# Two transformer layers of windowed attention and MLP on one core: half of the normed rows move to GpSimd, three tiles change their places, and all queues are ordered anew

## The chip, the cores and the metric

The kernel runs on one NeuronCore of a Trainium2 chip, with inputs and output in HBM. The metric is the device time of one execution in microseconds; lower is better. A profile is one execution taken by the hardware profiler; its time is given beside the times of the runs without a profile.

## The reference

The input is `x`, 2048 rows of 512 numbers in bf16. Two kinds of sublayer alternate, each on the normed rows and with a residual:

```python
def _layernorm(x, axis=-1, eps=1e-5):
    m = jnp.mean(x, axis=axis, keepdims=True)
    v = jnp.var(x, axis=axis, keepdims=True)
    return (x - m) / jnp.sqrt(v + eps)

def _A_ref(x, wqkv, wo):                     # H = 32 heads of 16, window W = 256
    q, k, v = ...                            # from x @ wqkv
    scores = jnp.einsum("bhqd,bhkd->bhqk", q, k) * (Dh ** -0.5)
    mask = (idx[:, None] - idx[None, :] >= 0) & (idx[:, None] - idx[None, :] < W)
    p = _softmax(jnp.where(mask[None, None], scores, -1e9), axis=-1)
    return ... @ wo                          # p times v, heads side by side

def _B_ref(x, w1, b1, w2, b2):               # F = 1792
    h = _gelu(jnp.einsum("bsd,df->bsf", x, w1) + b1)
    return jnp.einsum("bsf,fd->bsd", h, w2) + b2

x = x + _A_ref(_layernorm(x), wqkv, wo)
x = x + _B_ref(_layernorm(x), w1, b1, w2, b2)
x = x + _A_ref(_layernorm(x), wqkv, wo)      # the same weights once more
x = x + _B_ref(_layernorm(x), w1, b1, w2, b2)
```

## The kernel before

The 2048 rows are 16 tiles of 128; with the two repetitions there are 32 tile steps `tau`, in 16 blocks `b` of two tiles. All weights and `X`, the residual rows, stay in SBUF. For each block the program has these parts, each made of small nodes:

- `lnq(b)` and `kv(b)`: statistics of the rows (`bn_stats` L587, `bn_aggr` L589, variance plus eps L593, `pow` on GpSimd L599), the normed row `xn` (L609), a DMA transpose of it into `xnTA` (L614; six tiles use TensorE, L621), then the Q, K and V products (L635) and their copies out of PSUM into `QT` and `Va` (L576 on VectorE or L578 on ScalarE) and `KT` (L669). `Vs` is `Va` shifted by 64 partitions, made by two DMAs (L684).
- `attention(b)`: up to ten visits. A visit computes 512 columns of scores for eight heads (L736), two exponentials of 128x1024 out of PSUM into `E` on ScalarE (L743), and masks on `E`'s edges (L764, VectorE or GpSimd). Two P·V products (`pv`, L786) follow, each one after five visits; its result is transposed into `OD` (L795), divided by its sums (reciprocal L799, product into `Nb` L803) and transposed back (L809). The output projection adds to `X` (L835). Then a second norm gives the rows for the MLP, transposed into `xnTB`.
- `mlp(J)`: ten jobs of two or four tiles. Fourteen W1 products (L635, `xnTB` as moving data), bias and gelu into `gT` on ScalarE (L866, or L858 on VectorE and L861 on ScalarE in pairs), then one W2 product per tile (L635), added to `X` plus the bias row (L874 on GpSimd, L878 on VectorE). In the second repetition a DMA stores the tile (L882).

Nothing is scheduled at run time. A list `_ORDER` of 3080 node numbers gives one order for the whole program, and each engine's queue is that list cut down to its own nodes; `_ALT` lists the nodes that run on their second engine (a mask on GpSimd instead of VectorE, a copy on ScalarE instead of VectorE); `_BANKS` gives the PSUM bank of each group of matmuls. Every engine works through its queue in order and waits on semaphores for what a node reads or overwrites. One queue, SyncE's, issues all DMAs.

```python
for i in _ALT:
    nodes[i]["eng"], nodes[i]["fn"] = nodes[i]["alts"][1]
...
e0 = (first[b] + g) * 512 % NE              # the place of visit g of block b in E
```

`E` is a ring of `NE` columns, 15 visits. `xn` has four places. `xnTB` has two places of four tiles, by the job's number; `gT` holds one job of four tiles or two of two.

Of the kernel before, what the change touches and what calls it, by code (L numbers as in the profile page):

```python
# [7 lines left out]
ALU = mybir.AluOpType  # L8
# [11 lines left out]
class _Sched:  # L20
# [386 lines left out]
def bass_interleave_layers__sliding_block__dense_activation_gelu__prompt_kernel(  # L407
# [26 lines left out]
    SCALE = float(Dh) ** -0.5  # L434
    EPS = 1e-5
    VW = Dh + 1
    NB = NT // 2
    RB = T // 2
    HK = P // 2
    NE = 15 * 512  # L440
    VR = 8
    KB = 4
    QR = 3
    NXN = 4
    NOD = 1
    NXB = 3
# [10 lines left out]
    with ExitStack() as kctx:  # L457
# [368 lines left out]
        for J, (t0_, n_) in enumerate(JOBS):  # L826
            for i in range(n_):
                job_of[t0_ + i] = (J, i)
# [119 lines left out]
```

## Time and profile before

| what | value |
|---|---|
| median of 3 runs | 450.0 us (449.41 to 451.96) |
| profiled execution | 450.2 us, of which its span 448.5 us |
| TensorE matmul busy | 418.6 us, 93% of the span |
| ScalarE busy | 385.9 us, 86% |
| VectorE busy | 345.9 us, 77% |
| GpSimd busy | 207.6 us, 46% |
| TensorE clock granted | 0.995 of full speed |

In the profile PE is TensorE (PEld its weight loads), DVE VectorE, ACT ScalarE, POOL GpSimd and SP SyncE; an engine with a q at its end is its sequencer. L609 is line 609 of the kernel before. A group's row has the line, engine, operation, written and read tiles, their shapes and its count; then its busy time, the mean duration of one in ns, and the idle time of the engine before it with what ended it. A row of the timeline has its start, its duration and, in brackets, the idle time before it. Matmuls are pipelined, so that a busy TensorE isn't a TensorE at its peak.

### The profile page before, as it was taken

How to read it: one execution, taken by the hardware profiler on the slowest of the kernel's cores; microseconds unless marked ns; L12 is line 12 of the kernel's file. 1: busy time of each engine (PE TensorE's matmuls, PEld its weight loads, DVE VectorE, ACT ScalarE, POOL GpSimd, SP SyncE). 2: the span in 40 equal slices, each digit the busy share in tenths (PEclk: the TensorE clock that was granted, in tenths of full speed). 3: DMA queues.
4: the chain of work that ended last, by engine and by line, in shares of the span. 5: the costliest groups of instructions: out<-in, count | busy, mean ns of one | idle time of the engine just before them, and what ended most of it. 6: DMA issues, size and time to landing. Idle time of an engine off the chain costs nothing.

```text
span 448.5 us, 16830 instructions
## 1 busy us (share of the span) xinstructions
PE 418.6 (93%) x7507; PEld 231.5 (52%) x7579; DVE 345.9 (77%) x641; ACT 385.9 (86%) x455; POOL 207.6 (46%) x232
## 2 busy tenths in 40 slices
PE   7997999998789997999999999999899999999997
PEld 4554756544444553554445454464454464344673
DVE  6989989889885688786699778876797487763952
ACT  2896999999989898789899999999788978898632
POOL 5464343272542584641856136824555134734222
PEclk9999999999999999999999999999999999999999
DMA  7796412103210103221021201011422024101001
GB/s 236 200 201 174 100 33 50 26 15 49 49 31 13 26 4 52 50 26 23 4 54 40 43 13 27 22 33 30 70 56 44 1 33 80 38 1 48 5 23 48
DMA packets 47972, 23.25 MB, mean 52 GB/s; under 512 B 33180, under 2 KB 47900, under 8 KB 47900
## 3 DMA queue, kind: packets, MB, share of 16 engines
q1 hardware_dynamic: 47900, 22.17, 22.9%
q8 instruction: 60, 0.98, 0.9%
q14 instruction: 12, 0.10, 0.1%
HBM read 8.00 MB, written 2.10 MB: 23 GB/s over the span
## 4 chain that ended last, share of the span: by engine, by line
PE 69%; ACT 13%; DVE 10%; DMA 4%; issue 2%; SPq 1%; POOL 1%; DVEq 0%
PE ps L635 52%; ACT E L743 11%; PE ps L786 8%; PE ps L736 8%; DMA xnTB<-xn 2%; DVE OD L795 2%; DVE KT L669 2%; DVE xn L609 1%; DVE stat L587 1%; DVE E L764 1%; ACT gT L866 1%; DMA xnTA<-xn 1%; SPq L614 1%; DVE X L835 1%; POOL rstd L599 1%
## 5 line engine op out<-in xcount | busy, mean ns | idle before, releaser
L743 ACT ACTIVATE E<-ps 128x1024 bf16<-128x1024 f32 x300 | 285.0, 1035 | 34.7 <-PE ps L736 33.7
L764 POOL TENSOR_TENSOR E<-E,mask 128x512 bf16<-128x512 bf16 (+2 forms) x100 | 110.0, 1112 | 75.4 <-ACT E L743 75.2
L635 PE MATMUL ps<-xnTB,W_sb 128*128 128x512 bf16 (+1 forms) x542 | 114.0, 338 | 4.0 <-DMA xnTB<-xn 1.8
L635 PE MATMUL ps<-W_sb,gT 128*128 128x512 bf16 x420 | 111.3, 380 | 3.1 <-issue 2.4
L635 PE MATMUL ps<-xnTA,Wqkv_sb 128*128 128x256 bf16 x512 | 74.9, 273 | 3.5 <-issue 1.3
L635 PEld LDWEIGHTS ps<-xnTB,W_sb 128*128 128x128 bf16 x560 | 52.1, 98 | 43.8 <-issue 4.3
L764 DVE TENSOR_TENSOR E<-E,mask 128x512 bf16<-128x512 bf16 (+2 forms) x136 | 63.2, 490 | 11.4 <-ACT E L743 11.2
L736 PE MATMUL ps<-QT,KT 32*128 32x128 bf16 (+3 forms) x1920 | 60.5, 231 | 9.8 <-ACT E L743 5.9
L635 PEld LDWEIGHTS ps<-W_sb,gT 128*128 128x128 bf16 x448 | 39.7, 97 | 42.6 <-issue 3.8
L874 POOL TENSOR_TENSOR Xb<-X,b2all 128x512 f32<-128x512 bf16 x32 | 38.3, 1205 | 48.0 <-DVE X L878 44.5
L736 PEld LDWEIGHTS ps<-QT,KT 32*128 32x128 bf16 x1920 | 28.4, 92 | 61.1 <-ACT E L743 39.3
L635 PEld LDWEIGHTS ps<-xnTA,Wqkv_sb 128*128 128x128 bf16 x512 | 47.2, 98 | 24.5 <-issue 3.7
L795 DVE STREAM_TRANSPOSE OD<-ps 128x1024 f32<-128x1024 f32 x32 | 39.8, 1244 | 20.4 <-PE ps L786 19.9
L866 ACT ACTIVATE gT<-ps,b1T 128x512 bf16<-128x512 f32 (+1 forms) x80 | 43.5, 605 | 9.5 <-PE ps L635 9.1
L858 DVE TENSOR_SCALAR gT<-ps,b1T 128x512 bf16<-128x512 f32 (+1 forms) x60 | 36.7, 635 | 13.0 <-PE ps L635 12.7
L786 PE MATMUL ps<-E,Va 64*17 64x128 bf16 (+3 forms) x1920 | 43.6, 230 | 2.3 <-DMA Vs<-Va 0.8
L587 DVE BATCH_NORM_STATS2 stat<-X 128x6 f32<-128x512 bf16 x64 | 43.0, 680 | 1.9 <-DMA X<-in_A_x_dram 1.4
L786 PE MATMUL ps<-E,Vs 64*17 64x128 bf16 (+3 forms) x1920 | 44.2, 230 | 0.0
L803 POOL TENSOR_TENSOR Nb<-OD,Rc 128x512 bf16<-128x512 f32 x26 | 27.9, 1075 | 34.6 <-DVE Rc L799 33.7
L786 PEld LDWEIGHTS ps<-E,Va 64*17 64x17 bf16 x1920 | 37.1, 84 | 12.3 <-issue 8.3
L669 DVE TENSOR_TENSOR KT<-ps,parmask 128x1024 bf16<-128x1024 f32 x32 | 38.6, 1211 | 3.7 <-PE ps L635 3.6
L635 PE MATMUL ps<-Wo_sb,OT 128*128 128x512 bf16 x118 | 37.2, 380 | 1.2 <-issue 0.6
(51 smaller groups left out, 357.3 us busy)
## 6 DMA issues: line engine op xcount, KB each, us to landing
Vs<-Va SPq DMA_DIRECT2D x64, 68.0 KB, 2.1
W_sb<-in_B_w_dram SPq DMA_DIRECT2D x4, 512.0 KB, 7.7
out_dram<-X SPq DMA_DIRECT2D x16, 128.0 KB, 1.8
X<-in_A_x_dram SPq DMA_DIRECT2D x3, 512.0 KB, 6.0
Wqkv_sb<-in_A_wqkv_dram SPq DMA_DIRECT2D x4, 256.0 KB, 5.1
W_sb<-in_B_w_dram SPq DMA_DIRECT2D x2, 384.0 KB
W_sb<-in_B_w_dram SPq DMA_DIRECT2D x1, 768.0 KB, 8.0
Wqkv_sb<-in_A_wqkv_dram SPq DMA_DIRECT2D x1, 512.0 KB, 7.0
```

The lines of the kernel that those rows point to most:

```text
L587: add("dve", lambda e, B, t=t, k6=k6: e.bn_stats(stat6[:, k6, :], X[:, t, :]), reads=["X%d" % t], writes=["st%d" % k6], key="bs%d" % (k + j))
L635: r = e.matmul(ps[:, B[g][0], cols], lhsT, rhs, start=st, stop=sp)
L669: add("dve", lambda e, B, g=g, i=i: e.tensor_tensor(out=KT[:, kb, 2 * i : 2 * i + 2].rearrange("p c m a q -> p a (c m) q"), in0=ps[:, B[g] ...
L736: x = e.matmul(ps[:, bk[r], o : o + n], KT[rows, kb, c, m].rearrange("p a q -> p (a q)"), QT[rows, c, q : q + n], start=True, stop=True)
L743: add("act", lambda e, B, g_=g_, gi=gi: e.activation(E[:, 2 * gi : 2 * gi + 2, e0 : e0 + 512], ps[:, B[g_][0] : B[g_][0] + 2, :], AF.Exp, ...
L764: fn = lambda e, B: e.tensor_tensor(out=Ew, in0=Ew, in1=Mw, op=ALU.mult)
L786: x = e.matmul(ps[32 * r : 32 * r + VW, B[g][par], c % 2 * 2 * P + lo : c % 2 * 2 * P + hi], V[rows, (2 * b + m // 2) % VR, c * HC + 2 * r ...
L795: add("dve", lambda e, B: e.transpose(OD[:, s].rearrange("p a c q -> p (a c q)"), ps[:, B[g][0] : B[g][0] + 2, :]), reads=["ps:" + g], wri ...
L803: return e.tensor_tensor(out=Nb[:, s, :].rearrange("p (k a d) -> p a k d", a=2, d=Dh), in0=sums[:, :, :, 0:Dh], in1=rc[:, :, :, None].to_b ...
L858: add("dve", lambda e, B, g=g, fc=fc: e.tensor_scalar(out=gT[:, fc, c0 : c0 + M], in0=ps[:, B[g][0], 0:M], scalar1=b1T[:, fc : fc + 1], sc ...
L866: add("act", lambda e, B, g=g, fc=fc: e.activation(gT[:, fc, c0 : c0 + M], ps[:, B[g][0], 0:M], AF.Gelu_apprx_tanh, bias=b1T[:, fc : fc + ...
L874: add("pool", lambda e, B, t=t, xs=xs: e.tensor_tensor(out=Xb[:, xs, :], in0=X[:, t, :], in1=b2all[:], op=ALU.add), reads=["X%d" % t, "b2a ...
```

## The change

- The normed row (L609) gets GpSimd as a second engine. With the new `_ALT` 35 of the 64 rows are written by GpSimd and 29 by VectorE. In 21 pairs of tiles each engine writes one row, in seven pairs GpSimd writes both.
- `xnTB` is one tile of eight places, one for each tile step modulo 8, instead of two halves by job. `gT` has eight places instead of four, by the same rule.
- `E` has 11 visits instead of 15, and 64 columns of padding at the end of each row.
- `_ORDER`, `_ALT` and `_BANKS` are new. Of the other nodes with two engines, GpSimd does 115 masks instead of 100 and 24 divisions of P·V instead of 26; VectorE does 17 Q copies instead of 15, and four of the six copies of rows that TensorE transposed instead of three.

Matmuls, exponentials, gelu and DMAs are the same in number and shape.

```diff
 _ORDER = [
...
 _ALT = [
...
 _BANKS = [
...
-    NE = 15 * 512
+    NE = 11 * 512
...
-        xnTB = sb("xnTB", [P, 2, DC, 4 * P])
+        xnTB = sb("xnTB", [P, DC, 8 * P])
...
-        E = sb("E", [P, RG, NE])
+        E = sb("E", [P, RG, NE + HK])
...
-        gT = sb("gT", [P, FC, 4 * P])
+        gT = sb("gT", [P, FC, 8 * P])
...
-            add("dve", lambda e, B: e.tensor_scalar(
+            fx = lambda e, B: e.tensor_scalar(
                 out=xn[:, s, :], in0=X[:, t, :], scalar1=statmv[:, k, 0:1], scalar2=rstd[:, k : k + 1],
-                op0=ALU.subtract, op1=ALU.mult),
-                reads=["X%d" % t, "mv%d" % k, "rs%d" % k], writes=["xn%d" % s], key="xn%d" % k)
+                op0=ALU.subtract, op1=ALU.mult)
+            add("dve", fx, reads=["X%d" % t, "mv%d" % k, "rs%d" % k], writes=["xn%d" % s], key="xn%d" % k,
+                alt=(("pool", fx),))
...
-            layernorm(b, 1, [(xnTB[:, J % 2], i * P, "xb%d_%d" % (J % 2, i)) for J, i in (job_of[2 * b], job_of[2 * b + 1])])
+            layernorm(b, 1, [(xnTB, t % 8 * P, "xb%d" % (t % 8)) for t in (2 * b, 2 * b + 1)])
...
-            js = J % 2
             tau0, n = JOBS[J]
             M = n * P
-            h = J % 2 if n == 2 else 0
-            c0 = h * 2 * P
-            gn = lambda fc: ["g%d_%d" % (fc, i) for i in ((0, 1) if n == 4 else (h,))]
-            xr = ["xb%d_%d" % (js, i) for i in range(n)]
+            x0 = tau0 % 8 * P
+            c0 = x0
+            gn = lambda fc: ["g%d_%d" % (fc, (tau0 // 2 + i) % 4) for i in range(n // 2)]
+            xr = ["xb%d" % ((tau0 + i) % 8) for i in range(n)]
...
-                pe_group(g, [(W1_sb[:, dc, fc * P : (fc + 1) * P], xnTB[:, js, dc, 0:M], slice(0, M), dc == 0, dc == DC - 1)
+                pe_group(g, [(W1_sb[:, dc, fc * P : (fc + 1) * P], xnTB[:, dc, x0 : x0 + M], slice(0, M), dc == 0, dc == DC - 1)
```

More of the change, by code (lines that the diff above doesn't have):

```diff
@@ L821, in attention @@
                 outproj(2 * b + j)
-            layernorm(b, 1, [(xnTB[:, J % 2], i * P, "xb%d_%d" % (J % 2, i)) for J, i in (job_of[2 * b], job_of[2 * b + 1])])
+            layernorm(b, 1, [(xnTB, t % 8 * P, "xb%d" % (t % 8)) for t in (2 * b, 2 * b + 1)])
         od_rr = [0]
-        job_of = {}
-        for J, (t0_, n_) in enumerate(JOBS):
-            for i in range(n_):
-                job_of[t0_ + i] = (J, i)
         def outproj(tau):
```

361 rows, old and new, of tables (_ALT, _BANKS, _ORDER) are left out of this document.

## The prediction

> **What bounds the kernel now.** I read the page's busy times first, then the busy times of seven stretches whose borders are places where TensorE begins a P·V product (the last one of blocks 1, 2, 4, 5, 6 and 7), then the groups by form, then the timeline and the chain at the places where a stretch loses time.
>
> ```profile
> span 448.5 us, 16830 instructions
> PE 418.6 (93%) x7507; PEld 231.5 (52%) x7579; DVE 345.9 (77%) x641; ACT 385.9 (86%) x455; POOL 207.6 (46%) x232
> ```
>
> ```profile
> core 0: us, PE busy (x) PEld busy (x) DVE busy (x) ACT busy (x) POOL busy (x), PEclk, DMA share, GB/s
> 0.00:51.40 51.40, 44.52 (x696) 27.90 (x701) 45.76 (x88) 37.62 (x45) 26.28 (x43) 1.00 0.77 198
> 51.40:82.20 30.80, 30.34 (x547) 20.37 (x550) 27.50 (x55) 29.76 (x42) 11.38 (x13) 1.00 0.15 31
> 82.20:128.20 46.00, 38.71 (x908) 20.73 (x917) 38.82 (x74) 42.84 (x50) 21.39 (x24) 1.00 0.20 38
> 128.20:160.60 32.40, 31.77 (x511) 16.34 (x516) 20.81 (x39) 30.07 (x35) 13.95 (x16) 1.00 0.09 18
> 160.60:181.70 21.10, 17.57 (x425) 8.79 (x426) 16.64 (x30) 19.11 (x22) 13.50 (x15) 0.92 0.26 41
> 181.70:217.50 35.80, 34.38 (x567) 18.15 (x573) 26.84 (x50) 31.99 (x37) 17.34 (x18) 1.00 0.19 25
> 217.50:448.50 231.00, 221.29 (x3865) 119.18 (x3903) 169.49 (x309) 194.54 (x229) 103.74 (x105) 1.00 0.17 35
> ```
>
> The page says TensorE, 93% busy, and the stretches say where the other 7% lie. TensorE is idle 6.9 us of the first 51.4, where VectorE is the busiest engine (45.76); 7.3 us of 82 to 128 and 3.5 us of 161 to 182, where ScalarE is (42.84 of 46.00, 19.11 of 21.10): blocks 3, 4 and 6 have few MLP matmuls to lay beside the exponentials. From 217.5 on TensorE is busy 221.29 of 231.00 us, and no other engine comes near. So the matmuls, which are the same in number and shape in both kernels, are a floor, and what a new order can win lies in three stretches. An engine that isn't late in one of them gives nothing.
>
> **The memory edits.** Counted in the queues written into the two kernels, no more than eight visits' exponentials are alive at once, before as after; 11 slots hold them as 15 do, and every score matmul already stands behind the P·V product that frees its slot. When the first W1 matmul of a job stands in TensorE's queue, at most five W2 matmuls of the job before it are still to come (four after the change), so the doubled inner activations and the eight places of the W1 rows are hardly used. I cost these at 0 and their cover is TensorE's own queue order; if I have overlooked a slot, a score would wait for one P·V product, about 1.4 us, and not repeatedly.
>
> **The normed rows.** VectorE loses 35 of 64, GpSimd gets them. In the same new plan GpSimd takes 15 more masks (115 for 100), VectorE two more divisions of P·V (8 for 6) and two more Q copies, ScalarE two fewer Q copies and one fewer copy of transposed rows.
>
> ```profile
> L609 DVE TENSOR_SCALAR xn<-X,statmv,rstd 128x512 bf16<-128x512 bf16 x64 | 28.5, 462 | 6.4 <-POOL rstd L599 4.8 <-DMA xnTA<-xn 0.9 <-DVE Va L576 0.6
> L764 POOL TENSOR_TENSOR E<-E,mask 128x512 bf16<-128x512 bf16 x51 | 59.6, 1171 | 30.8 <-ACT E L743 30.8
> L764 DVE TENSOR_TENSOR E<-E,mask 128x512 bf16<-128x512 bf16 x65 | 30.9, 488 | 4.8 <-ACT E L743 4.7
> L576 DVE CAST Va<-ps 128x512 bf16<-128x512 f32 x25 | 16.9, 683 | 2.6 <-PE ps L635 2.6
> L578 ACT ACTIVATE Va<-ps 128x512 bf16<-128x512 f32 x7 | 4.3, 610 | 0.0
> L593 POOL TENSOR_SCALAR rstd<-statmv 128x2 f32<-128x2 f32 x24 | 6.1, 252 | 53.9 <-DVE statmv L589 53.9
> L516 POOL TENSOR_SCALAR_AFFINE_SELECT mask<-mask 128x64 bf16<-128x64 bf16 x3 | 0.7, 236 | 0.1
> L521 POOL TENSOR_SCALAR mask<-mask 128x128 bf16<-128x128 bf16 x1 | 0.3, 297 | 0.1
> L501 POOL TENSOR_SCALAR_AFFINE_SELECT ident<-ident 128x128 bf16<-128x128 bf16 x1 | 0.3, 292 | 0.0
> ```
>
> No row shows the normed row on GpSimd. Below: its two small TENSOR_SCALAR rows (252 ns at 2 elements, 297 at 128) rise 0.36 ns an element, which gives 0.43 us at 512. Above: the mask of the same size with two inputs, 1.17 us. The one-input AFFINE_SELECT rows (236 at 64, 292 at 128) rise 0.88 ns an element and give 0.63 us. I take 0.65, since that is the row with the same traffic, one tile in and one out; both ends stay for the range. On GpSimd that makes 35 × 0.65 = 23 us and 15 × 1.17 = 18 us more, about 248 of 448 us: no bound as a whole. The Trainium skill ("GPSIMD Engine Reference", § 3.1 Elementwise — side-by-side cycle accounting) has a one-input loop at 1.03 cycles an element; an estimate from that page is 0.44 us and a start-up, which speaks for the lower half; no run so far shows it for this shape.
>
> First stretch. Up to the place where VectorE evacuates the last P·V of block 1, its new queue holds six normed rows fewer (6 × 0.46 = 2.8 us), two masks fewer (1.0), one V copy more (0.68) and two or three small instructions (0.3): 2.8 us less. What it would bring is seen where TensorE waits for VectorE:
>
> ```profile
> 34.64 2.08 DVE L764 TENSOR_TENSOR E<-E,mask 128x512 bf16<-128x512 bf16 x2
> 38.71 1.19 DVE L669 TENSOR_TENSOR KT<-ps,parmask 128x1024 bf16<-128x1024 f32 x1
> 39.99 0.41 DVE L609 TENSOR_SCALAR xn<-X,statmv,rstd 128x512 bf16<-128x512 bf16 x1
> 41.48 1.73 DVE L609 TENSOR_SCALAR xn<-X,statmv,rstd 128x512 bf16<-128x512 bf16 x2
> ...
> 34.33 1.64 POOL L764 TENSOR_TENSOR E<-E,mask 128x768 bf16<-128x768 bf16 x1 [2.08 <-ACT E L743]
> 40.75 1.15 POOL L764 TENSOR_TENSOR E<-E,mask 128x512 bf16<-128x512 bf16 x1 [0.87 <-ACT E L743]
> 41.86 1.20 POOL L874 TENSOR_TENSOR Xb<-X,b2all 128x512 f32<-128x512 bf16 x1
> ...
> 39.96 1.48 PE L635 MATMUL ps<-xnTA,Wqkv_sb 128*128 128x256 bf16 x10 [1.27 <-DVE KT L669]
> 44.99 0.26 PE L736 MATMUL ps<-QT,KT 32*128 32x192 bf16 x3 [0.26 <-DVE KT L669]
> ```
>
> The matmul at 39.96 waits 1.27 us for the K copy of 38.71. Two masks there took 2.08 us instead of 2 × 0.49, and two normed rows 1.73 instead of 2 × 0.41, both while GpSimd worked on SBUF tiles: a VectorE instruction of these kinds starts as it should and then holds on until GpSimd's is over. That cuts both ways. The change takes those rows off VectorE, but 21 of the 32 pairs are now split, one row on each engine, let go by the same `pow` on GpSimd. GpSimd, whose own queue it is, goes first, and VectorE's row then lasts 0.65 + 0.41, no less than the two did on VectorE. Stepping through the new queues there: GpSimd's masks stand without a break up to the end of the one of 34.33 (35.97), so VectorE's mask before the residual add again ends near 36.4 (34.64 + 2.08 = 36.72 now), the K copy starts at 38.5 (38.71), the split pair delays the evacuation after it by 0.6, but the two rows at 41.48 are gone. So the stretch gains between 2.8 us (all of it passes) and -0.6 us (all of it is lost to this). I take the middle, 1.2 us. What comes early in the stretch is handed on in full: from 51.4 to 82.2 TensorE is busy 30.34 of 30.80, then ScalarE holds the pace, and both only start sooner. In the stretch 82 to 128 the new ScalarE queue holds the same work, so its 7.3 us of idle TensorE stay.
>
> 160.6 to 181.7. ScalarE is the bound and loses one V copy there, 0.61 us, to VectorE, which is busy 16.64 of 21.10 and so has room for 0.68: gain 0.6. The two rows that the next MLP job waits for are split as above, at no gain.
>
> SyncE. One wait in the TensorE-bound part is a queue matter:
>
> ```profile
> 316.84 0.95 DVE E L764
> 317.79 1.09 SPq L882
> 318.93 1.20 SPq L614
> 320.18 2.04 DMA Vs<-Va
> 322.26 1.44 PE ps L786 x120
> ...
> 322.26 0.28 PE L786 MATMUL ps<-E,Va 64*17 64x256 bf16 x4 [0.82 <-DMA Vs<-Va]
> ```
>
> The shifted copy of V is issued behind an output store (L882) and a transpose (L614), and P·V of block 12 idles 0.82 us for it. In the new SyncE queue the second store stands after that copy, the transpose still before it. The copy is issued some 1.1 us sooner, and the wait goes: 0.8 us. Next late there would be its masks; the last of them that the chain shows ends at 317.79, well before.
>
> Sum: 1.2 + 0.6 + 0.8 = 2.6 us. The profiled execution took 450.2 us, 448.5 of them its span; 450.2 - 2.6 = **447.6 us**. Against the median of 450.0 that is 0.5% less. About 0.5% (2.25 us) is what a measurement of this kernel can tell from no change.
>
> **The rivals.** *All of it passes*: the 2.8 us, the 0.6, the 0.8, and about 1 of the 7.3 us in 82 to 128, where VectorE (38.82 of 46.00 busy) has five normed rows fewer and frees PSUM sooner: 450.2 - 5.2 = 445.0. For it: VectorE's load falls in every stretch. Against: the port waits above.
>
> *Nothing changes*: VectorE's gain is eaten by waits for GpSimd, other small waits move about, 450. For it: after 217.5 us there is nothing to win but 9.7 us of small gaps, and none is VectorE's alone.
>
> *Slower: the split pairs and GpSimd's in-order queue.* The mechanism is the one of 41.48: VectorE's row costs up to 1.24 us instead of 0.41, its masks too. If GpSimd's row costs 1.17, the four rows in front of GpSimd's masks for the first blocks push these 4 × (1.17 - 0.65) = 2.1 us back, the first P·V products of block 1 wait for them, and four split pairs add 4 × 0.83 = 3.3 us where 2.8 were saved: the first stretch gets 2.6 us longer, 82 to 128, with two or three more split pairs, about 1 us, and the other gains don't come: 450.2 + 3.6 = 453.8. It decides from about 1.0 us for GpSimd's row, or 0.8 us as the mean of VectorE's. For it: GpSimd gets busier just where it is in front of masks. The Trainium skill ("SBUF — State Buffer", § SBUF: two separate sides) states the rule behind it: the pair of ports that both engines use is locked for a whole instruction, and the other one blocks. By that rule, the trace agrees: 1.73 us for two rows of 0.41. Against it: half of VectorE's rows, which suffer from this, are gone.
>
> **How the numbers follow.** Forecast 0.42 (its own range 445.5 to 449.5, a little over half of it below 447.75), all passes 0.18, nothing 0.17, slower 0.23. Faster by over 0.5%: 0.24 + 0.18 = 0.42; within: 0.18 + 0.17 = 0.35; slower: 0.23. The range goes from 444.0, just under the best case, to 453.8, the slower case's own time; half of that case and a few per cent below are left out.
>
> **What would show it.** In the changed profile: 29 rows of L609 on VectorE and 35 on GpSimd at 0.43 to 1.17 us; the seven stretches, by their P·V products, with the first ending near 50.2 us, 82 to 128 as long as now, 161 to 182 0.6 shorter, and P·V of block 12 without a wait for Vs. A first stretch over 52 us, or VectorE rows of 0.8 us and more, says the port; a stretch after 217 that changes by over 2 us says that the order of the matmuls matters in a way which I don't see.

## The result, and the profile after

| | before | after |
|---|---|---|
| median | 450.98 us of 4 runs (449.41 to 452.58) | 464.49 us of 4 runs (464.08 to 465.64) |
| ratio | | 1.0317, 95% interval 1.0283 to 1.0350 |
| profiled execution | 450.2 us, span 448.5 | 464.22 us, span 462.5 |

The change makes the kernel 3.2% slower. The forecast was 447.6 us, and 464.5 lies outside its range. Ratios here and below leave out the runs in which the chip was in a slower state, one of the four of a_head_fast and two of the ten of a_old_tables. The page of the changed kernel, busy times first:

```profile
span 462.5 us, 16921 instructions
PE 429.9 (93%) x7579; PEld 231.2 (50%) x7579; DVE 345.9 (75%) x597; ACT 385.8 (83%) x452; POOL 294.8 (64%) x279
```

GpSimd has 87 us more than before (207.6), where the prediction expected 41. VectorE lost 35 rows and 15 masks and is as busy as before, since what stayed with it takes longer (below). (TensorE's two sums can't be compared: 72 of its 7579 matmul records are missing in the trace of before.) The seven stretches of the changed kernel, with borders at the same P·V products as those of before:

```profile
core 0: us, PE busy (x) PEld busy (x) DVE busy (x) ACT busy (x) POOL busy (x), PEclk, DMA share, GB/s
0.00:55.90 55.90, 45.43 (x701) 27.54 (x701) 45.57 (x84) 39.51 (x47) 44.00 (x53) 0.97 0.62 169
55.90:88.80 32.90, 32.38 (x556) 21.11 (x557) 26.02 (x48) 28.10 (x40) 15.53 (x15) 0.95 0.29 55
88.80:137.60 48.80, 41.19 (x918) 20.84 (x918) 41.82 (x72) 42.59 (x49) 28.09 (x25) 0.97 0.16 33
137.60:170.80 33.20, 32.42 (x524) 16.39 (x529) 21.25 (x36) 30.23 (x35) 25.48 (x22) 1.00 0.09 18
170.80:189.70 18.90, 16.02 (x426) 8.42 (x425) 17.40 (x32) 17.86 (x21) 14.91 (x14) 1.00 0.22 45
189.70:226.10 36.40, 35.70 (x577) 18.45 (x576) 25.17 (x42) 32.66 (x37) 25.47 (x23) 1.00 0.12 25
226.10:462.50 236.40, 226.78 (x3904) 118.43 (x3903) 168.62 (x285) 194.82 (x229) 141.36 (x130) 1.00 0.15 34
```

Against before the stretches are 4.5, 2.1, 2.8 and 0.8 us longer, 2.2 shorter, 0.6 and 5.4 longer: 14.0 together. The first, where a gain of 1.2 us was forecast, loses most, and GpSimd is busy 44.00 of its 55.90 us (26.28 of 51.40 before).

A part of this stands in the column PEclk, TensorE's granted clock. In the changed kernel's trace it falls to 0.5 at three places, for some 3.4 us each: from 26.0 and 56.7 us, behind the two waits for GpSimd's masks that the timeline below shows, and from 128.6 us, behind a wait of 1.04 us for a mask of VectorE. In the trace of before it falls once, from 177.9 us. What the lower clock takes away is 5.0 us in all against 1.7, so 3.3 of the 14.0 us. In the second stretch, in which TensorE hardly rests, it is 1.6 of the 2.1 us. Not every wait is followed by such a fall; the longest of the timeline below, 2.99 us, isn't.

The groups by form say what GpSimd is busy with:

```profile
L612 POOL TENSOR_SCALAR xn<-X,statmv,rstd 128x512 bf16<-128x512 bf16 x35 | 74.5, 2131 | 5.1 <-DMA xnTA<-xn 3.4
L768 POOL TENSOR_TENSOR E<-E,mask 128x512 bf16<-128x512 bf16 x63 | 73.5, 1167 | 44.1 <-ACT E L747 44.0
L768 DVE TENSOR_TENSOR E<-E,mask 128x512 bf16<-128x512 bf16 x53 | 29.9, 568 | 1.8 <-ACT E L747 1.5
L612 DVE TENSOR_SCALAR xn<-X,statmv,rstd 128x512 bf16<-128x512 bf16 x29 | 16.2, 566 | 12.2 <-POOL rstd L602 7.8 <-DMA xnTA<-xn 3.3 <-DVE E L768 1.0
```

L612 is the normed row (L609 before). One takes GpSimd 2131 ns, where the prediction took 650 and had 1170 as its upper end. The masks on GpSimd cost what they did (1167, before 1171). In the waits, TensorE's weight load for P·V (L786 before, L790 after) now stands for a GpSimd mask, which it hardly did; the columns are the total in us, the number of waits and the longest:

```profile
PEld ps L786 <- POOL E L764: 0.8, 2, 0.4
```

```profile
PEld ps L790 <- POOL E L768: 5.9, 3, 2.5
```

The first fence is before, the second after. The timeline of the changed kernel shows what stands ahead of these masks, and at the end how the W1 products of a later MLP job come late:

```profile
18.52 4.15 POOL L612 TENSOR_SCALAR xn<-X,statmv,rstd 128x512 bf16<-128x512 bf16 x2
22.64 1.79 POOL L768 TENSOR_TENSOR E<-E,mask 128x768 bf16<-128x768 bf16 x1
...
24.48 0.28 PE L790 MATMUL ps<-E,Va 64*17 64x256 bf16 x4 [1.91 <-POOL E L768]
...
50.50 2.08 POOL L612 TENSOR_SCALAR xn<-X,statmv,rstd 128x512 bf16<-128x512 bf16 x1
52.54 1.46 POOL L807 TENSOR_TENSOR Nb<-OD,Rc 128x512 bf16<-128x512 f32 x1
53.96 1.89 POOL L768 TENSOR_TENSOR E<-E,mask 128x512 bf16<-128x512 bf16 x2
...
51.42 1.67 DVE L768 TENSOR_TENSOR E<-E,mask 128x512 bf16<-128x512 bf16 x4
...
55.91 0.09 PEld L790 LDWEIGHTS ps<-E,Va 64*17 64x17 bf16 x4 [2.46 <-POOL E L768]
...
341.20 4.14 POOL L612 TENSOR_SCALAR xn<-X,statmv,rstd 128x512 bf16<-128x512 bf16 x2
...
343.35 4.16 SPq L618 DMA_TRANSPOSE xnTB<-xn  x2
...
348.70 1.67 PE L639 MATMUL ps<-xnTB,W_sb 128*128 128x512 bf16 x7 [2.99 <-issue]
```

Two rows hold GpSimd for 4.15 us, the mask of block 0 starts behind them at 22.64, and TensorE idles 1.91 us until 24.48. A row, a division and two masks end at 55.85, and the P·V product that ends the first stretch starts at 55.91, after its weight load has waited 2.46 us. From 341.20 on both rows of one pair are written by GpSimd, one after the other. Their transposes follow, the second of them is issued at 345.37 and takes up to 3.2 us to land, and W1 waits 2.99 us until 348.70.

### The profile page after: what moved, and what is told of

Read it like the earlier page. It is cut to its first block, busy times and chain, and to the rows that moved or that the text cites. A ratio compares the mean times of both kernels' runs of the same rounds, so it can differ in the third digit from the quotient of the medians.

```text
span 462.5 us, 16921 instructions
## 1 busy us (share of the span) xinstructions
PE 429.9 (93%) x7579; PEld 231.2 (50%) x7579; DVE 345.9 (75%) x597; ACT 385.8 (83%) x452; POOL 294.8 (64%) x279
## 5 line engine op out<-in xcount | busy, mean ns | idle before, releaser
L768 POOL TENSOR_TENSOR E<-E,mask 128x512 bf16<-128x512 bf16 (+2 forms) x115 | 126.4, 1111 | 65.8 <-ACT E L747 65.5
L639 PE MATMUL ps<-xnTB,W_sb 128*128 128x512 bf16 (+1 forms) x560 | 118.6, 341 | 4.5 <-issue 3.0
L639 PE MATMUL ps<-W_sb,gT 128*128 128x512 bf16 x448 | 120.3, 380 | 0.0
L639 PE MATMUL ps<-xnTA,Wqkv_sb 128*128 128x256 bf16 x512 | 76.8, 279 | 4.6 <-DVE OD L799 1.6
L612 POOL TENSOR_SCALAR xn<-X,statmv,rstd 128x512 bf16<-128x512 bf16 x35 | 74.5, 2131 | 5.1 <-DMA xnTA<-xn 3.4
L768 DVE TENSOR_TENSOR E<-E,mask 128x768 bf16<-128x768 bf16 (+2 forms) x121 | 67.1, 576 | 7.0 <-ACT E L747 6.6
L790 PE MATMUL ps<-E,Va 64*17 64x128 bf16 (+3 forms) x1920 | 44.0, 232 | 9.1 <-DVE E L768 2.7
L857 DVE TENSOR_SCALAR gT<-ps,b1T 128x512 bf16<-128x512 f32 (+1 forms) x60 | 37.0, 637 | 14.1 <-PE ps L639 13.5
L790 PEld LDWEIGHTS ps<-E,Va 64*17 64x17 bf16 x1920 | 36.8, 84 | 19.0 <-issue 7.5
L790 PE MATMUL ps<-E,Vs 64*17 64x128 bf16 (+3 forms) x1920 | 44.7, 232 | 0.0
L807 POOL TENSOR_TENSOR Nb<-OD,Rc 128x512 bf16<-128x512 f32 x24 | 25.9, 1079 | 23.0 <-DVE Rc L803 17.7
```

The lines of the kernel that those rows point to most:

```text
L612: fx = lambda e, B: e.tensor_scalar(out=xn[:, s, :], in0=X[:, t, :], scalar1=statmv[:, k, 0:1], scalar2=rstd[:, k : k + 1], op0=ALU.subtra ...
L639: r = e.matmul(ps[:, B[g][0], cols], lhsT, rhs, start=st, stop=sp)
L768: fn = lambda e, B: e.tensor_tensor(out=Ew, in0=Ew, in1=Mw, op=ALU.mult)
L790: x = e.matmul(ps[32 * r : 32 * r + VW, B[g][par], c % 2 * 2 * P + lo : c % 2 * 2 * P + hi], V[rows, (2 * b + m // 2) % VR, c * HC + 2 * r ...
L857: add("dve", lambda e, B, g=g, fc=fc: e.tensor_scalar(out=gT[:, fc, c0 : c0 + M], in0=ps[:, B[g][0], 0:M], scalar1=b1T[:, fc : fc + 1], sc ...
```

## The experiments

The questions were, first, whether the loss comes from the rows on GpSimd, from the new order or from the new places; then why a row costs 2.1 us; and last, what the plan is worth at the price that was assumed. "After" and "before" are the two kernels; ratios are to the kernel before on the same chip. Its medians there were 450.6 to 451.6 us.

**a_rows_dve.** After, all 64 normed rows on VectorE.

```diff
-_ALT = [..., 110, 156, 158, 241, ...]   # the 35 nodes of the rows among them
+_ALT = [...]                            # without them
```

> The changed kernel with all 64 normed rows on VectorE again, everything else (order, masks, places) as changed. Theory 1, that the 14 us come from the normed row's duration on GpSimd (2.13 us, not 0.65): the 35 x 2.13 = 74.5 us leave GpSimd, VectorE gets 35 x 0.41 = 14 us back, and the time is that of before or a little less, 446 to 452. Theory 2, that the new order and the 15 masks more on GpSimd are slow by themselves: 460 or more. Theory 3, that the new places of E, xnTB and gT cost something: 460 or more as well.

457.31 us, ratio 1.0140 (1.0072 to 1.0208). This is the number of none of the three theories. Taking the rows away from GpSimd recovers about half of the loss. What the other half is, this run alone doesn't show; the new queues then hold VectorE rows that weren't there when the order was made.

**b_rows_pool.** Before, with the same 35 rows on GpSimd and nothing else.

```diff
-            add("dve", lambda e, B: e.tensor_scalar(
+            fx = lambda e, B: e.tensor_scalar(
...
+            add("dve", fx, ..., alt=(("pool", fx),))
+_ALT = [...]                            # before's, and the 35 rows
```

> The kernel before with the same 35 normed rows on GpSimd, nothing else changed (old order, old masks, old places). Theory 1: the rows alone slow it at least as much as the change did, since its order isn't made for them: 464 to 475. Theories 2 and 3: under 456, since the new order and the new places aren't in it.

465.15 us, ratio 1.0333 (1.0253 to 1.0412), as theory 1 had it: the rows alone cost as much as the whole change. Its groups by form and its waits:

```profile
L610 POOL TENSOR_SCALAR xn<-X,statmv,rstd 128x512 bf16<-128x512 bf16 x35 | 76.9, 2200 | 1.4
```

```profile
PE ps L637 <- DMA xnTB<-xn: 5.7, 2, 3.4
PE ps L637 <- DMA xnTA<-xn: 2.5, 1, 2.5
PE ps L623 <- POOL xn L610: 2.2, 1, 2.2
PE ps L788 <- POOL E L766: 2.1, 3, 1.0
```

Here it is the products that use the late rows which wait (10.4 us in the first three lines, where the kernel before has 2.2), more than P·V behind late masks (2.1).

**a_const.** After, GpSimd's 35 rows subtract and multiply constants instead of the mean and the reciprocal deviation.

```diff
+            fp = lambda e, B: e.tensor_scalar(
+                out=xn[:, s, :], in0=X[:, t, :], scalar1=0.125, scalar2=0.5, op0=ALU.subtract, op1=ALU.mult)
...
-                alt=(("pool", fx),))
+                alt=(("pool", fp),))
```

> The changed kernel, whose 35 rows on GpSimd subtract and multiply by constants instead of by the row's mean and rstd (this leaves the norm of these rows out; queues, waits and shapes stay). If the two scalars read per partition make the 2.13 us, the row falls to between 0.43 and 0.65 us, and theory 1 says 446 to 450, what the prediction's sum says. If the row's duration stays at 2.1 us, two operations on 512 elements cost that on GpSimd whatever the scalars, and the time stays at 464. Theory 2: 460 or more whatever the row costs.

461.49 us, ratio 1.0223 (1.0164 to 1.0282), and a row still costs 1.94 us:

```profile
L615 POOL TENSOR_SCALAR xn<-X 128x512 bf16<-128x512 bf16 x35 | 67.6, 1937 | 5.6 <-DMA xnTA<-xn 3.6
```

So the scalars, one per partition, are a small part of the price: 0.19 us of 2.13, and 3 us of the time.

**a_old_tables.** After's tiles and places with before's three tables.

```diff
-_ORDER, _ALT, _BANKS = after's
+_ORDER, _ALT, _BANKS = before's
```

> The changed kernel's tiles (11 visits in E with padding, eight places of xnTB and gT) with the order, the engines and the banks of the kernel before. Theory 3: the places cost time, 455 or more. Theories 1 and 2: 450 within 0.5%, as the prediction has it (places at 0).

450.94 us, ratio 0.9973 (0.9930 to 1.0017). The eight places and the 11 slots cost nothing that can be seen, 0.2% at most; the theory that they bring waits has fallen.

**a_forms.** After, GpSimd's 35 rows in seven forms, five rows each: subtract and multiply or multiply and add with constants, multiply and add in either order with a value per partition, and single operations. The norm is left out on these rows.

```diff
+            XNP = [2, 4, 5, 7, 8, 9, 11, ...]               # the rows that GpSimd writes
+            q = XNP.index(k) % 7
+            # 0: -0.125, *0.5   1: *0.5, +0.0625   2: -0.125   3: *rstd
+            # 4: *rstd, +mean   5: +mean, *rstd    6: *0.5
```

> The changed kernel, in which the 35 rows on GpSimd take seven forms in turn, five rows each: subtract and multiply with constants; multiply and add with constants; subtract alone; multiply by a per-partition scalar alone; multiply and add with two per-partition scalars; add and multiply with two; multiply by a constant alone (the norm is left out of these rows; only the duration of each form is read). Theory 1a, that the order of operations subtract-then-multiply has no fast path on GpSimd while multiply-then-add has: 2.0 us for the first, 0.4 to 0.8 us for the second and fifth. Theory 1b, that any two operations on 512 elements cost 1.9 us: all two-operation forms at 1.9 to 2.1, the single ones at about 1. Theory 1c, that it is one element after the other whatever is done: all seven near 1.9.

One execution, 456.39 us. The timeline has the first row of the first six forms, in the order 0, 2, 1, 3, 4, 5:

```profile
10.44 1.95 POOL L618 TENSOR_SCALAR xn<-X 128x512 bf16<-128x512 bf16 x1
...
19.79 1.50 POOL L619 TENSOR_SCALAR xn<-X 128x512 bf16<-128x512 bf16 x1
21.36 0.62 POOL L618 TENSOR_SCALAR xn<-X 128x512 bf16<-128x512 bf16 x1
...
25.65 1.57 POOL L619 TENSOR_SCALAR xn<-X,rstd 128x512 bf16<-128x512 bf16 x1
...
41.52 0.89 POOL L618 TENSOR_SCALAR xn<-X,rstd,statmv 128x512 bf16<-128x512 bf16 x1
44.47 0.77 POOL L618 TENSOR_SCALAR xn<-X,statmv,rstd 128x512 bf16<-128x512 bf16 x1
```

Over the five rows of each form: subtract then multiply 1.93 to 1.95 us with constants, multiply then add 0.62. With a value per partition multiply and add take 0.76 to 0.89 us in either order, against 2.13 for subtract and multiply in the changed kernel. The price hangs on which operations are paired, as theory 1a had it, and multiply and add are fast in either order. No form pairs a subtraction in another way, so whether every pair with a subtraction is slow stays open. That a single operation takes 1.50 to 1.85 us, over twice the fast pair, was foreseen by none of the theories.

**a_old_engines** and **b_new_engines.** The order of one kernel with the engines of the other, all rows on VectorE: after with before's `_ALT`, and before with after's `_ALT` less the 35 rows.

```diff
-_ALT = after's            # a_old_engines
+_ALT = before's
...
-_ALT = before's           # b_new_engines
+_ALT = after's, without the 35 rows
```

> The changed kernel with its new order and banks, but every node on the engine that it had before: all rows on VectorE, 100 masks on GpSimd instead of 115, 26 divisions, 17 Q copies on ScalarE. With rows on VectorE alone the new order took 457.3. Theory A, that the 15 masks and other engines make the rest of the loss: 450 to 453. Theory B, that the order of the queues makes it, which counts on a VectorE freed of 35 rows: 455 to 460.

> The kernel before with its own order, but the changed kernel's engines for masks, divisions and copies (115 masks on GpSimd); rows stay on VectorE. Theory A: 454 to 458. Theory B: 449 to 453.

464.28 us, ratio 1.0289 (1.0236 to 1.0342), and 465.01, ratio 1.0313 (1.0247 to 1.0379). Both times lie above what either theory gave. Either half alone costs 13 to 14 us, without one slow row, though both halves together with cheap rows cost 1 or 2 us (below). So the order and the choice of engines belong together, and these two runs can't say which of them is the better one. In a_old_engines TensorE waits 3.5 us for VectorE's V copies and 3.0 for its K copies, where the kernel before waits 1.9 for K copies and hardly for V; why these arise stays open.

**a_fast_const.** After, GpSimd's 35 rows as a multiplication and an addition with constants; the norm is left out on them. The plan then runs at the price that the prediction assumed.

```diff
+            fp = lambda e, B: e.tensor_scalar(
+                out=xn[:, s, :], in0=X[:, t, :], scalar1=0.5, scalar2=0.0625, op0=ALU.mult, op1=ALU.add)
...
-                alt=(("pool", fx),))
+                alt=(("pool", fp),))
```

> The changed kernel, whose 35 rows on GpSimd multiply and add constants, the form that took 0.62 us (the norm of these rows is left out); all else as changed. That is the duration that the prediction put in (0.65). Theory 1 alone (the price is the only step that failed): 446 to 449, with no wait of the first P.V products for GpSimd's masks. Theory 2 (the new plan loses time even at this price, by masks that GpSimd took over): 452 to 456.

451.87 us, ratio 1.0037 (1.0005 to 1.0069). Its group by form, and its first stretch up to the same P·V product:

```profile
L615 POOL TENSOR_SCALAR xn<-X 128x512 bf16<-128x512 bf16 x35 | 22.4, 640 | 6.0 <-DMA xnTA<-xn 3.2
```

```profile
0.00:50.70 50.70, 44.71 (x701) 27.51 (x702) 44.36 (x83) 37.39 (x44) 33.68 (x53) 1.00 0.73 188
```

At 640 ns a row the loss of 13.5 us is gone but for 1. That lies between the two theories, just below the 452 of theory 2, though no P·V product waits for a GpSimd mask any more, as theory 1 had it. The first stretch gains 0.7 us, where the kernel with slow rows loses 4.5.

**a_fast.** After, with the norm kept: a small instruction for each pair of tiles writes the negated means, and GpSimd adds and multiplies.

```diff
+                    e.tensor_scalar(out=nmean[:, k + j : k + j + n, None], in0=statmv[:, k + j : k + j + n, 0:1],
+                                    scalar1=-1.0, scalar2=0.0, op0=ALU.mult, op1=ALU.add)
...
+            fp = lambda e, B: e.tensor_scalar(
+                out=xn[:, s, :], in0=X[:, t, :], scalar1=nmean[:, k : k + 1], scalar2=rstd[:, k : k + 1], op0=ALU.add, op1=ALU.mult)
```

> The changed kernel, correct, with the rows on GpSimd as add and multiply by two per-partition scalars (0.77 us in the forms' run); the negated mean comes from one more small instruction beside each variance plus eps (33 in all, 0.25 us on GpSimd or 0.16 on VectorE). GpSimd: 35 x 1.3 = 46 us less than with the change, 6 more for the small ones. Theory 1: 448 to 452. Theory 2: 454 to 458.

452.22 us, ratio 1.0028 (1.0001 to 1.0055), the row at 0.84 us:

```profile
L618 POOL TENSOR_SCALAR xn<-X,nmean,rstd 128x512 bf16<-128x512 bf16 x35 | 29.3, 839 | 5.3 <-DMA xnTA<-xn 3.6
```

That is just above theory 1. This is the change as it should be written: 12 us better than as it was made, and no better than the kernel before.

**b_rows_fast.** Before's order and engines, the 35 rows on GpSimd as in a_fast_const.

> The kernel before, its own order and engines, with the 35 rows on GpSimd in the form that takes 0.62 us (multiply and add constants; the norm is left out of them). With the same rows in the slow form it took 465. Theory P (price): the slow form's extra 35 x 1.5 us on GpSimd made that, so 450 to 454. Theory M (mismatch): an order made for other engines loses some 13 us whatever the row costs, as the two runs with exchanged engines did, so 461 to 466.

450.09 us, ratio 0.9996 (0.9950 to 1.0041), as theory P had it. Against b_rows_pool only the operations differ, and 15 us go. It says a second thing: VectorE is rid of more than half of its rows, and within that interval the time doesn't move. Its group and its first stretch:

```profile
L613 POOL TENSOR_SCALAR xn<-X 128x512 bf16<-128x512 bf16 x35 | 23.5, 671 | 3.4 <-DMA xnTA<-xn 0.6
```

```profile
0.00:51.20 51.20, 44.69 (x701) 28.00 (x701) 43.54 (x80) 37.48 (x45) 30.77 (x50) 1.00 0.76 199
```

VectorE is busy 2.2 us less in the first stretch than before (45.76), and the stretch ends 0.2 us sooner.

**a_head_fast.** After, with the cheap form on only the seven rows 2, 4, 5, 7, 8, 9 and 32.

```diff
+            fp = fx if k not in (2, 4, 5, 7, 8, 9, 32) else lambda e, B: e.tensor_scalar(
+                out=xn[:, s, :], in0=X[:, t, :], scalar1=0.5, scalar2=0.0625, op0=ALU.mult, op1=ALU.add)
```

> The changed kernel with the 0.62 us form in the seven rows of the first stretch alone (rows 2, 4, 5, 7, 8, 9 and 32; their norm is left out), the other 28 rows stay at 2.1 us. In the trace of the changed kernel TensorE had lost 4.5 us by the last P.V product of block 1, 9.4 by that of block 4 and 13.7 at the end. Theory P with losses that add up: about 464.5 - 5 = 459 to 460. If a late start is only waited for later anyway: 463 or more. If all hangs on the start: 453 or less.

454.50, 456.78 and 458.10 us, ratio 1.0113 (1.0042 to 1.0184); there is no profile for these. Seven of the 35 rows account for about 8 us by the medians, 9 by the ratios, of the 12.6 between the slow and the cheap rows: more than their number, and more than the 5 that were expected.

**b_store_later.** Before, with the second output store moved behind the shifted copy of V in the order.

> The kernel before with one thing moved: the second output store is issued behind the shifted V copy of tile 24 instead of before it, as in the changed order. The prediction's term: P.V of block 12 loses its wait of 0.8 us, the stretch from the last P.V of block 11 to it goes from 10.4 to about 9.6 us, and the time falls by 0.8 us, less than the comparison of times can tell. If a mask or a score is late there anyway, the stretch stays at 10.2 or more.

449.69 us, ratio 0.9970 (0.9927 to 1.0013). The timeline of SyncE and TensorE (L660 is the V copy, L858 the store, L762 P·V):

```profile
315.83 0.59 SPq L660 DMA_DIRECT2D Vs<-Va  x1
316.46 2.09 SPq L590 DMA_TRANSPOSE xnTA<-xn  x1
318.59 0.59 SPq L660 DMA_DIRECT2D Vs<-Va  x1
319.28 0.53 SPq L858 DMA_DIRECT2D out_dram<-X  x1
...
320.72 0.28 PE L762 MATMUL ps<-E,Va 64*17 64x256 bf16 x4 [0.19 <-DMA Vs<-Va]
```

The wait of 0.82 us at P·V of block 12 is down to 0.19. From the start of the last P·V product of block 11 to that of the first of block 12 it takes 9.7 us, before 10.3: most of the step is there, though the whole kernel's interval still includes no change.

## Why the prediction was wrong, point by point

**The failed step: GpSimd's row at 0.65 us.** It measured 2.13, nearly twice the upper bound of 1.17. That bound was a mask of the same size with two inputs, taken as a ceiling for a row with one; 0.65 itself came from the AFFINE_SELECT rows, and two small TENSOR_SCALAR rows gave the lower end, 0.43. None of these rows subtracts and multiplies; the larger TENSOR_SCALAR row (L521, 297 ns) multiplies and adds. On the same instruction and traffic a_forms shows a factor of 3 between these two pairs of operations. For multiply and add 0.65 would have been right: 0.64 us in a_fast_const, and GpSimd busy 243.3 us there against a forecast of 248. That hit is partly luck, since 0.65 came from another instruction and the row that does multiply and add led to 0.43. The Trainium skill's figure ("GPSIMD Engine Reference", § 3.1 Elementwise — side-by-side cycle accounting), from which 0.44 us and a start-up was estimated, names no operations. The 0.44 us lies 0.18 below multiply and add with constants here, and 1.5 below subtract and multiply.

With the row's length the time follows, all in after's plan: 0.64 us 451.9, 0.84 us 452.2, 1.94 us 461.5, 2.13 us 464.5. Of the 52 us that GpSimd's rows last longer than at 0.64 (35 × 1.49), 12.6 arrive at the end, about a quarter. In the two traces 3.3 us of the difference stand in the lower clock.

**The slower rival** had the right side and half of the mechanism: rows in front of GpSimd's masks in its in-order queue, P·V behind the masks, and a turning point from about 1.0 us. It gave 453.8 because it stopped at 1.17 us. (By the prediction's own rule a split row would then last 1.17 + 0.41 = 1.58 us on VectorE, not 1.24, which makes 455.2; that changes nothing.) The half on the ports fell for the slow row, and so the first stretch of over 52 us, which the prediction would have read as the port, wasn't one. GpSimd's row of 50.50 ends at 52.58; the four masks that VectorE begins at 51.42, by the view of that tile in the changed kernel (shortest, median and longest in ns, first and last start):

```profile
L768 DVE TENSOR_TENSOR E<-E,mask x4: 393/484/552, 51.4 to 52.5; 128x512 bf16<-128x512 bf16 x2, 128x768 bf16<-128x768 bf16 x2
```

None lasts over 552 ns, and the fourth begins while the row still runs. By the rule of the Trainium skill quoted there ("SBUF — State Buffer", § SBUF: two separate sides), the first of these masks would have lasted until 52.58; for this instruction the trace doesn't agree, while it did for those of before.

The whole trace says the same, when VectorE's masks of 128x512 are sorted by what GpSimd did as they began: 11 began during a slow row and have a median of 415 ns, 29 while GpSimd was idle and have 416, and the four that began during a mask of GpSimd lasted 1167 to 1866. That VectorE's masks have a mean of 568 ns over the whole kernel, against 488 before, thus comes from GpSimd's masks and its other instructions with two inputs, and not from the rows. Of VectorE's own rows two began during a row of GpSimd; they lasted 0.62 and 0.80 us, not 2.5. The fast row is another matter: in b_rows_fast the two masks of 128x512 that began during one lasted 786 and 830 ns.

**The first stretch, -1.2 us.** +4.5 in the changed kernel. At the assumed price -0.7 in a_fast_const and -0.6 in a_fast, inside the bounds of -2.8 and +0.6. So the working isn't contradicted but for its price; the middle of so wide a range was a choice.

**The memory edits at 0.** Right: a_old_tables, 0.9973 (0.9930 to 1.0017).

**160.6 to 181.7, -0.6 us.** The stretch got 2.2 us shorter, but the row can't be read as that: before's execution had a granted clock of 0.92 just there, after's 1.00. At a clock of 1.00 before's order takes 19.4 us from P·V to P·V in b_rows_fast and 19.3 in a_old_tables, the changed order 18.9 and, in a_fast_const, 19.2. That is a gain of 0.1 to 0.5 us, from one execution each.

**SyncE, -0.8 us.** Right in place and nearly in size: in b_store_later 0.6 of the 0.8 us of waiting go. In the changed kernel the same piece, from block 11 to block 12, takes 9.3 us instead of 10.3 and is lost among the rest.

**The sum at its own price.** A second step failed, a smaller one. Even with 0.64 us a row the plan takes 451.9 us where the kernel before takes 450.8 on the same chip: 1 us more instead of 2.6 less, so some 4 us were missing besides the price. The second stretch and the last hold them. The first two rows are those of a_fast_const, the other two those of b_rows_fast, which has before's order at the same price:

```profile
50.70:82.80 32.10, 31.30 (x550) 20.22 (x549) 27.08 (x50) 30.22 (x43) 12.01 (x15) 1.00 0.30 55
217.90:453.60 235.70, 227.91 (x3904) 118.76 (x3903) 166.14 (x285) 194.68 (x229) 124.19 (x130) 0.99 0.16 34
...
51.20:82.10 30.90, 30.89 (x560) 20.43 (x559) 26.11 (x53) 29.86 (x42) 13.03 (x15) 1.00 0.15 31
216.20:447.30 231.10, 226.49 (x3904) 119.25 (x3903) 167.25 (x297) 194.56 (x229) 112.07 (x117) 1.00 0.17 35
```

The new order takes 1.2 and 4.6 us more there. The profiled execution of a_fast_const is the longest of its eleven runs (455.4 us): a W1 product waits 2.4 us for its transposed rows, the one that waits 2.99 in the changed kernel, and the clock falls behind it. But a_fast, where that wait is 0.3 us and the last stretch has a clock of 1.00, still takes 32.5 and 234.2 us, 1.6 and 3.1 more than b_rows_fast. In its last stretch the waits of TensorE that the timeline lists add up to 3.7 us, 1.6 of them at one place, 326.69 us, for VectorE's transposition into `OD`; in b_rows_fast they are 0.8. The prediction looked for what the new order could win and put what it could lose in the stretches bound by TensorE at nothing, without stepping through them; its own sign for this, a stretch after 217 that changes by over 2 us, came true.

The prediction also read 9.7 us of small gaps from the last stretch of before. About half of them are missing matmul records: with before's order and all records b_rows_fast has TensorE idle 4.6 us there.

And b_rows_fast shows that moving 35 rows from VectorE to GpSimd brings nothing in before's order. At the assumed price the rival "nothing changes" would have been the right case. Why order and engines of different kernels lose 13 us together remains open.

## What to carry to other kernels

Before work moves to another engine, time one instruction of exactly that form there: operation pair, kinds of scalars, shape. Rows of other operations, with the same traffic or more, put this price at 0.65 us and at most 1.17 where it was 2.13, and rewriting subtract as the addition of a negated value took it to 0.84. And relief of an engine counts only where others wait for that engine's end: at a fair price more than half of VectorE's normed rows could be moved here, and the time stayed where it was. A new order is to be stepped through also where it has nothing to win, for what it can lose.

## What the runs showed of the hardware

On GpSimd the same TENSOR_SCALAR of 128x512 in bf16 took 0.62 us as multiply and add with constants, 0.76 to 0.89 as a pair of multiply and add with values per partition, 1.50 to 1.85 as a single operation, and 1.93 to 2.13 as subtract and multiply. One operation is thus slower than this pair; whether an addition of nothing behind a multiplication helps, no run shows.

During slow rows VectorE's masks went on (median 415 ns, and 416 beside an idle GpSimd), while those that began during a mask of GpSimd lasted 1167 to 1866 ns in the same trace, and two that began during a fast row in b_rows_fast 786 and 830.

TensorE's granted clock fell to 0.5 for some 3.4 us behind some of its waits and not behind others: three times in the trace of the changed kernel, once in that of before, never in that of b_rows_fast. Why it fell here and not there, no run shows.
